# The front of a three-layer kernel, emitted from a list of nodes instead of a hand-written step table

## The chip, the cores and the metric

One core of a Trainium2 chip runs the whole program. Its engines work side by side, each through its own row of instructions in a fixed order: TensorE (PE: matmul and transpose, results go to PSUM), VectorE (DVE), ScalarE (ACT), GpSimd (POOL) and the queue engine SyncE (SP). An instruction that waits holds up everything behind it on its engine. The metric is the device time of one execution in microseconds. The runs shown have a median of 1156.69 us (1154.55 to 1157.05).

## What is computed

Three layers follow each other. A long convolution by Fourier transform over 8 batches of 3072 tokens with 256 channels; a mixture of 8 experts, where each token goes to the expert with the largest logit as long as that expert has room (768 places); and a feed-forward layer with softplus. Tokens that found no room are rows of zeros for the last layer.

```python
X = np.fft.rfft(x, axis=1)
y = np.fft.irfft(X * F, n=x.shape[1], axis=1)
...
expert_idx = np.argmax(logits, axis=1)
gate_w = probs[np.arange(N), expert_idx]
for i in range(N):
    e = expert_idx[i]
    if counts[e] < capacity:
        disp[e, counts[e]] = x[i]
h = np.maximum(np.einsum('ecd,edf->ecf', disp, w1), 0.0)
y = np.einsum('ecf,efd->ecd', h, w2)
...
h = x @ w_in
g = np.maximum(h, 0.0) + np.log1p(np.exp(-np.abs(h)))
return (g @ w_out).astype(np.float32)
```

## The kernel before

Only the first three batches are transformed unless an expert still has room after them. The transform of a batch is four matrix stages. Batch 0 keeps stage 1 on the chip (`x1`, `tr1`); batches 1 and 2 write it to memory (`x1_out`, tile `s`, buffer `mid`) and read it back reordered (`load_i`, tile `it`). `s2` is the second stage: two matmuls into a PSUM tile of the ring `y`, three VectorE products with the filter (L237 to L240), and a GpSimd sum (L241). `s3` is the third stage, whose result ScalarE copies into the tile `e`. `gsum`, `gturn` and `gate` make the logits, the gate weights `ga` and the place of each token. `tr2` and `s4` do the last stage and scale it, and `park` writes the rows to memory (`rowsd`).

`table` turns the places of a batch into an index table by one-hot matmuls. It has four chunks. For each, VectorE compares into `lo` and `hv` (L369, L370), GpSimd multiplies `hv` by the token numbers (L371), TensorE does eight matmuls (L375), and VectorE adds the result into `ts` (L377). There is one buffer of `lo` and of `hv`.

After that come 16 units of 384 places, two for each expert. A unit gathers its rows (`load_x`), transposes them (`tr_x`, tiles `xh`, `xl`), and does `w1`, `w2` in eight tasks each, with every operand split in a high and a low part. The result `yh`, `yl` goes through 16 softplus steps: `wi` (six matmuls into `pi`, L593), three ScalarE instructions, a VectorE sum `g` (L496), a split into `gh`, `gl`, and `wo` (nine matmuls, L616). `wih`, `wil`, `woh`, `wol` are the last layer's weights, which arrive as 64-bit numbers. 16 conversions (`split_res`) turn them into 32-bit numbers and split them. A conversion is five VectorE instructions (L473 to L481) with a ScalarE instruction between the third and the fourth. Its scratch is a PSUM tile (`pv`) as long as a ring is given, and an SBUF tile (`wv`) after that.

The program is recorded as it is written, so the order of the calls is the order in each engine's row. The order is a hand-written table of steps: `ev(t, order, fn)` puts a call on step t, and step 0 is the first softplus step. Batch b starts at step -71 plus 0, 17 or 29, and each function has a fixed offset from there. Most functions hold their TensorE part and the copy of its result together. Memory is handed over in rooms: `x_done`, `make_room`, `low_room` and `finish` close the pools of the transform and open those of the units.

Of the kernel before, what the change touches and what calls it, by code (L numbers as in the profile page):

```python
# [25 lines left out]
WI0 = 4  # L26
STATIC = 3

# [68 lines left out]

def body(tc, cap, x, ff, fx, wg, w1, w2, win, wout, m1, m2, m4, small, out):
# [25 lines left out]
    wexp = sm[0:N1, 576:832].rearrange("p (n e) -> p n e", e=E)  # L124
    eoff = sm[0:N1, 832:840]
    tok1 = sm[0:N1, 840:872]
    iota = sm[0:N1, 872:]
# [4 lines left out]
    slead = const.tile([128, nblk], F32, name="slead")  # L132
    flag = const.tile([1, 1], I32, name="flag")
# [4 lines left out]
    class Conv:  # L138


        def __init__(self, st, ste, stf, stx, tag):
# [18 lines left out]
            self.ga = {}  # L160
            self.e = {}
# [12 lines left out]
        def make_m3(self, q):  # L174
            ps = psa.tile([128, 4, 128], F32, name="p0", tag="a")
            for i in range(4):
                nc.tensor.transpose(ps[:, i], self.m2s[:, 4 * q + i], ident)
            nc.scalar.copy(self.m3s[:, 4 * q:4 * q + 4], ps)
# [11 lines left out]
        def x1(self, b, g, h):  # L190

            if g == 0 and h == 0:
                self.d = self.ep[1].tile([128, 2, N1, N2], F32, name="d", tag="e1")
            xt = self.xt[b, g]
            ps = psa.tile([128, 4, N1], F32, name="p1", tag="a")
            for i in range(4):
                nc.tensor.matmul(ps[:, i], lhsT=xt[:, i, 128 * h:128 * h + 128], rhs=self.m1s, start=True, stop=True)
            (nc.scalar.copy, nc.vector.tensor_copy)[h](
                self.d[:, h, :, 4 * g:4 * g + 4].rearrange("c q n -> c n q"), ps)

        def tr1(self, b, k):

            ps = psa.tile([128, 2, 2, 128], F32, name="p2", tag="a")
            for i in range(2):
                for h in range(2):
                    p = 2 * k + i
                    nc.tensor.transpose(ps[:, i, h], self.d[:, h, 4 * p:4 * p + 4].rearrange("c r n -> c (r n)"), ident)
            self.it[b, k] = self.ip.tile([128, 2, D], F32, name="it", tag="it")
            nc.scalar.copy(self.it[b, k], ps.rearrange("p i h c -> p i (h c)"))

        def x1_out(self, b, g):

            xt = self.xt.pop((b, g))
            t = self.sp.tile([N1, 4, D], F32, name="s1", tag="s1")
            for i in range(2):
                ps = psa.tile([N1, 2, D], F32, name="p8", tag="a")
                nc.tensor.matmul(ps.rearrange("q n c -> q (n c)"), lhsT=self.m1s,
                                 rhs=xt[:, 2 * i:2 * i + 2].rearrange("p n c -> p (n c)"), start=True, stop=True)
                nc.scalar.copy(t[:, 2 * i:2 * i + 2], ps)
            nc.scalar.dma_start(mid[b - 1].rearrange("(q n) c -> q n c", n=N2)[:, 4 * g:4 * g + 4], t)  # L220
# [6 lines left out]
        def s2(self, b, k):  # L227

            p0 = 2 * k
            it = self.it.pop((b, k))  # L230
            ps = psy.tile([128, 2, D], F32, name="p3", tag="y")
            for i in range(2):
                nc.tensor.matmul(ps[:, i], lhsT=self.m2s[:, p0 + i], rhs=it[:, i], start=True, stop=True)
# [6 lines left out]
            nc.vector.tensor_tensor(out=t2[64:128], in0=ps[0:64], in1=fi, op=ALU.mult)  # L240
            nc.gpsimd.tensor_tensor(out=z, in0=z, in1=t2, op=ALU.add)  # L241
            self.z[b, k] = z

        def s3(self, b, k):

            if k == 0:
                self.e[b] = self.ep[b % 2].tile([128, 2, N1, N2], F32, name="e", tag=f"e{b % 2}")
            z = self.z.pop((b, k))
            ps = pso.tile([128, 2, 2, 128], F32, name="p4", tag="o")
            for i in range(2):  # L250
                for h in range(2):
                    nc.tensor.matmul(ps[:, h, i], lhsT=z[:, i, 128 * h:128 * h + 128], rhs=self.m3s[:, 2 * k + i],
                                     start=True, stop=True)
            nc.scalar.copy(self.e[b][:, :, 8 * k:8 * k + 8].rearrange("c h q n -> c h (q n)"),
                           ps.rearrange("c h i x -> c h (i x)"))

        def tr2(self, b, m):

            ps = psa.tile([N1, 4, 128], F32, name="p5", tag="a")
            for i in range(4):  # L260
                nc.tensor.transpose(ps[:, i], self.e[b][:, i % 2, :, 2 * m + i // 2], ident)
            self.jt[b, m] = self.jp.tile([N1, 2 * D], F32, name="j", tag="j")
            (nc.vector.tensor_copy if b == STATIC - 1 and m % 2 else nc.scalar.copy)(
                self.jt[b, m], ps.rearrange("p a c -> p (a c)"))

        def gsum(self, b):

            gx = self.gp.tile([128, N1, 8], F32, name="gx")
            for half in range(2):
                ps = pso.tile([128, N1 // 2, 8], F32, name="pg", tag="o")  # L270
                qs = slice(48 * half, 48 * half + 48)
                for hc in range(2):
                    for j in range(4):
                        nc.tensor.matmul(ps[32 * j:32 * j + 32], lhsT=self.wgs[:, hc],
                                         rhs=self.e[b][:, hc, qs, 8 * j:8 * j + 8],
                                         start=(hc == 0), stop=(hc == 1), skip_group_check=True)
                (nc.vector.tensor_copy, nc.scalar.copy)[half](gx[:, qs], ps)
            self.gx = gx

        def gturn(self, b):  # L280

            self.gsb[b] = self.gp.tile([N1, N2, E], F32, name="gsb", tag="gsb")
            gv = self.gsb[b].rearrange("p (j t a) e -> p t a j e", t=2, a=4)
            for t in range(2):
                ps = psa.tile([N1, 4, 128], F32, name="p7", tag="a")
                for a in range(4):
                    nc.tensor.transpose(ps[:, a], self.gx[:, :, 4 * t + a], ident)
                nc.vector.tensor_copy(gv[:, t], ps.rearrange("p a (j x) -> p a j x", x=32)[:, :, :, 0:E])

        def s4(self, b, m):  # L290

            g, i0 = m // 2, m % 2 * 2
            if i0 == 0:
                self.yt[b, g] = self.yp.tile([N1, 4, D], F32, name="yt", tag="yt")
            ps = pso.tile([N1, 2, D], F32, name="p6", tag="o")
            nc.tensor.matmul(ps.rearrange("p a c -> p (a c)"), lhsT=self.m4s, rhs=self.jt.pop((b, m)),
                             start=True, stop=True)
            for i in range(2):
# [3 lines left out]
        def gate(self, b):  # L302


            gp = self.gp
            pl = pso.tile([N1, N2, E], F32, name="pl", tag="o")
            nc.tensor.matmul(pl.rearrange("p n e -> p (n e)"), lhsT=self.m4s,
                             rhs=self.gsb[b].rearrange("p n e -> p (n e)"), start=True, stop=True)
            mx = gp.tile([N1, N2], F32, name="mx")
            nc.vector.tensor_reduce(out=mx, in_=pl, axis=AXL.X, op=ALU.max)  # L310
            dl = gp.tile([N1, N2, E], F32, name="dl")
            nc.vector.tensor_tensor(out=dl, in0=pl, in1=mx.unsqueeze(2).to_broadcast([N1, N2, E]), op=ALU.subtract)
# [695 lines left out]
```

## Time and profile before

| what | value |
|---|---|
| profiled execution | 1156.95 us, span of the trace 1154.8 us |
| TensorE busy, mean granted clock | 1071.3 us (93%), 0.958 |
| ScalarE, GpSimd, VectorE busy | 780.4 us (68%), 600.5 us (52%), 488.2 us (42%) |
| HBM over the span | 102 GB/s |
| first softplus matmul | 343.5 us |

The busy share of TensorE is an average over two halves, the front before the first softplus step and the units after it, and has to be read for each. Matmuls are pipelined, so their durations overlap: the work of a task is the time from its start to the start of the next. A granted clock of 1.00 is 2.4 GHz, of 0.50 it is 1.2 GHz.

### The profile page before, as it was taken

How to read it: one execution, taken by the hardware profiler on the slowest of the kernel's cores; microseconds unless marked ns; L12 is line 12 of the kernel's file. 1: busy time of each engine (PE TensorE's matmuls, PEld its weight loads, DVE VectorE, ACT ScalarE, POOL GpSimd, SP SyncE). 2: the span in 40 equal slices, each digit the busy share in tenths (PEclk: the TensorE clock that was granted, in tenths of full speed). 3: DMA queues.
4: the chain of work that ended last, by engine and by line, in shares of the span. 5: the costliest groups of instructions: out<-in, count | busy, mean ns of one | idle time of the engine just before them, and what ended most of it. 6: DMA issues, size and time to landing. Idle time of an engine off the chain costs nothing. (4 is left out here: it accounts for less than half of the span.)

```text
span 1154.8 us, 18098 instructions
## 1 busy us (share of the span) xinstructions
PE 1071.3 (93%) x6704; PEld 994.9 (86%) x6704; DVE 488.2 (42%) x848; ACT 780.4 (68%) x1618; POOL 600.5 (52%) x548
## 2 busy tenths in 40 slices
PE   9999876865878999999999999999999999999994
PEld 7746664533778999999999999999999999999994
DVE  4538876465765364332333333333232333232221
ACT  3656332652557878777787878787777777777883
POOL 0313423242566555567657475665757566554553
PEclk9999887877899999999999999999999999999997
DMA  9977321453351124543323233333211122100000
GB/s 280 276 221 224 106 69 37 127 169 101 114 174 51 37 60 152 200 136 120 119 101 128 93 128 106 114 106 115 65 46 65 51 60 60 51 15 11 14 15 16
DMA packets 71953, 119.30 MB, mean 103 GB/s; under 512 B 6832, under 2 KB 45872, under 8 KB 71856
## 3 DMA queue, kind: packets, MB, share of 16 engines
q1 hardware_dynamic: 58032, 89.74, 24.2%
q10 hardware_dynamic: 9216, 15.73, 4.4%
q0 software_dynamic: 4608, 12.59, 3.3%
q8 instruction: 54, 0.88, 0.3%
q14 instruction: 43, 0.35, 0.1%
HBM read 70.85 MB, written 47.19 MB: 102 GB/s over the span
## 5 line engine op out<-in xcount | busy, mean ns | idle before, releaser
L496 DVE SCALAR_TENSOR_TENSOR g<-pi,ln 128x384 f32<-128x384 f32 x256 | 142.7, 557 | 509.5 <-ACT ln L491 469.5
L408 POOL TENSOR_TENSOR gl<-g,gh 128x384 fp32r<-128x384 f32 x256 | 259.8, 1019 | 117.2 <-ACT gh L407 90.1
L616 PE MATMUL po<-woh,gh 128*128 128x256 f32 x768 | 219.1, 285 | 2.7 <-DVE ot L623 1.3
L616 PE MATMUL po<-wol,gh 128*128 128x256 f32 x768 | 217.0, 282 | 0.0
L616 PE MATMUL po<-woh,gl 128*128 128x256 f32 x768 | 216.6, 282 | 0.0
L488 ACT ACTIVATE ab<-pi 128x384 f32<-128x384 f32 x256 | 124.4, 486 | 124.9 <-PE pi L593 118.8
L593 PE MATMUL pi<-yh,wih 128*128 128x384 f32 x512 | 172.7, 337 | 5.1 <-DVE g L496 5.1
L593 PE MATMUL pi<-yh,wil 128*128 128x384 f32 x512 | 173.9, 340 | 0.0
L593 PE MATMUL pi<-yl,wih 128*128 128x384 f32 x512 | 172.8, 338 | 0.0
L408 POOL TENSOR_TENSOR w1l<-ws,w1h 128x512 fp32r<-128x512 f32 x64 | 83.5, 1305 | 154.1 <-ACT w1h L407 151.8
L616 PEld LDWEIGHTS po<-woh,gh 128*128 128x128 f32 x768 | 145.0, 189 | 3.7 <-ACT ab L488 1.9
L616 PEld LDWEIGHTS po<-wol,gh 128*128 128x128 f32 x768 | 145.6, 190 | 0.0
L616 PEld LDWEIGHTS po<-woh,gl 128*128 128x128 f32 x768 | 145.5, 189 | 0.0
L491 ACT ACTIVATE ln<-ab 128x384 f32<-128x384 f32 (+1 forms) x257 | 135.0, 525 | 8.2
L489 ACT ACTIVATE ab<-ab 128x384 f32<-128x384 f32 (+1 forms) x257 | 134.7, 524 | 8.1
L407 ACT CAST gh<-g 128x384 fp32r<-128x384 f32 x256 | 130.0, 508 | 0.3 <-DVE g L496 0.3
L241 POOL TENSOR_TENSOR z<-z,t 128x512 f32<-128x512 f32 x36 | 52.8, 1468 | 138.8 <-DVE t L240 97.0
L408 POOL TENSOR_TENSOR w2l<-ws,w2h 128x512 fp32r<-128x512 f32 x64 | 82.8, 1294 | 56.7 <-ACT w2h L407 55.3
L593 PEld LDWEIGHTS pi<-yh,wih 128*128 128x128 f32 x512 | 96.9, 189 | 5.9 <-DVE g L496 5.9
L565 ACT ACTIVATE hh<-pw 128x384 fp32r<-128x384 f32 x128 | 63.0, 492 | 53.8 <-PE pw L561 53.8
L593 PEld LDWEIGHTS pi<-yh,wil 128*128 128x128 f32 x512 | 96.9, 189 | 0.0
L578 PE MATMUL py<-hh,w2h 128*128 128x384 f32 x256 | 89.8, 351 | 7.5 <-DVE yl L585 7.5
(148 smaller groups left out, 2030.8 us busy)
## 6 DMA issues: line engine op xcount, KB each, us to landing
ws<-in_w_dram SPq DMA_DIRECT2D x128, 256.0 KB, 2.8
out_dram<-cs SPq DMA_DIRECT2D x48, 512.0 KB, 3.8
xt<-in_x_dram SPq DMA_DIRECT2D x24, 384.0 KB, 8.4
mid<-s ACTq DMA_DIRECT2D x16, 384.0 KB, 3.3
it<-mid ACTq DMA_DIRECT2D x24, 256.0 KB, 3.2
rowsd<-yt SPq DMA_DIRECT2D x16, 384.0 KB, 3.2
wst<-in_win_dram SPq DMA_DIRECT2D x8, 512.0 KB, 5.5
wst<-in_wout_dram SPq DMA_DIRECT2D x8, 512.0 KB, 4.0
```

The source lines that it names most:

```text
L241: nc.gpsimd.tensor_tensor(out=z, in0=z, in1=t2, op=ALU.add)
L407: nc.scalar.copy(dst_hi, src)
L408: nc.gpsimd.tensor_tensor(out=dst_lo, in0=src, in1=dst_hi.bitcast(F32), op=ALU.subtract)
L488: nc.scalar.activation(out=ab[:, :n], in_=h, func=ACTF.Abs)
L489: nc.scalar.activation(out=ab[:, :n], in_=ab[:, :n], func=ACTF.Exp, scale=-1.0)
L491: nc.scalar.activation(out=ln[:, :n], in_=ab[:, :n], func=ACTF.Ln, bias=1.0)
L496: nc.vector.scalar_tensor_tensor(out=g[:, :n], in0=h, scalar=0.0, in1=ln[:, :n], op0=ALU.max, op1=ALU.add)
L565: nc.scalar.activation(out=hh, in_=ps, func=ACTF.Relu)
L578: nc.tensor.matmul(self.py[d], lhsT=a[:, j % 2, ds], rhs=b, start=(j == 0 and n == 0), stop=(j == 7 and n == 2))
L593: nc.tensor.matmul(self.pi, lhsT=a[i // 2][:, i % 2, k], rhs=b[:, k], start=(n == 0), stop=(n == 5))
L616: nc.tensor.matmul(self.po[t], lhsT=a[:, ts], rhs=b[:, i], start=(i == 0 and n == 0), stop=(i == KI - 1 and n == 2))
```

## The change

The part of the program before the first softplus step is no longer a table of steps. Each call becomes a node with an engine, a cost in ns, its predecessors, the buffer rings it takes and gives back, and the bytes it moves. `Plan.order` walks through the list when the program is built: it keeps a clock for each engine, for the transfers and for the port of VectorE and GpSimd, and places next the node that can start first (starts within 60 ns of the engine's clock count as equal), of equals the one with the longest chain behind it. `LIFT` is a table of lengths added for ten groups of nodes. The functions are cut so that a TensorE part and the copy of its result are separate nodes. The table gets eight chunks with two sets of `lo` and `hv` that live in the constants; `wexp` is broadcast instead of stored. `woh` and `wol` go into the left room together, and the tiles `yh`, `yl` take the low room. Conversions that the plan starts after the end of its TensorE nodes are put on steps of the second half, with SBUF scratch.

```diff
+QT = 8
...
+    BUFS = {"a": 3, "y": 2, "o": 3, "it": 4, "z": 3, "t2": 2, "j": 4, "yt": 3, "xt": 8, "s1": 2, "e0": 1, "e1": 1,
+            "gx": 1, "gsb": 1, "lo": 2, "wst": 3, "wf": 2, "ws": 5, "w1h": 3, "w2h": 3, "xd": 3, "x": 2, "h": 4, "Y": 3}
...
+    def add(self, name, engine, cost, fn, after=(), take=(), give=(), nbytes=0, lock=False, tail=0, behind=()):
+        assert name not in self.node
+        self.node[name] = (engine, cost, fn, list(after), list(take), list(give), nbytes, lock, tail, list(behind))
...
+        while ready:
+            best = None
+            for n, r in ready.items():
+                f = free[node[n][0]]
+                t = when(n, max(r, f))
+                if t is None:
+                    continue
+                if node[n][7]:
+                    t = max(t, port)
+                key = max(t, f + 60), -length[n]
+                if best is None or key < best[0]:
+                    best = key, n, t
...
+            start[n], free[e] = t, t + cost
+            done[n] = t + cost + self.HOP[e]
+            if lock:
+                port = t + cost
+            if nbytes:
+                bus = max(bus, t + cost + 1200) + nbytes / 285
+                done[n] = bus + 600
...
-            for q in range(4):
-                ns = slice(8 * q, 8 * q + 8)
...
-                ps = psa.tile([128, nblk], F32, name="p9", tag="a")
-                for j in range(8):
-                    nc.tensor.matmul(ps, lhsT=lo[:, j], rhs=hv[:, j], start=(j == 0), stop=(j == 7))
...
+        def table_d(self, b, q):
...
+            n = N2 // QT
+            lo, hv = onehot[q % 2]
+            ns = slice(n * q, n * q + n)
+            for row, w, to in ((0, 128, lo), (1, nblk, hv)):
+                nc.vector.tensor_tensor(out=to, in0=iota[:, 0:w].unsqueeze(1).to_broadcast([N1, n, w]),
+                                        in1=ij[b][:, row, ns].unsqueeze(2).to_broadcast([N1, n, w]), op=ALU.is_equal)
...
+        def table_p(self, b, q):
+            n = N2 // QT
+            lo, hv = onehot[q % 2]
+            ps = self.ps["t", b, q] = psa.tile([128, nblk], F32, name="p9", tag="a")
+            for j in range(n):
+                nc.tensor.matmul(ps, lhsT=lo[:, j], rhs=hv[:, j], start=(j == 0), stop=(j == n - 1))
...
+            for k in range(12):
+                load(("it", b, k), lambda b=b, k=k: cv.load_i(b, k), 256, "ACT",
+                     after=[("mid", b, g) for g in range(8)], take=["it"],
+                     behind=[("it", b, k - 1) if k else ("tr1", 11) if b == 1 else ("it", b - 1, 11)])
...
+                add(s2, "PE", 862, lambda b=b, k=k: cv.s2(b, k), after=[("it", b, k), ("m2", k // 2)], take=["y"],
+                    give=[("it", ("it", b, k) if b else ("tr1", k))], behind=prev("s2"))
+                add(tf, "DVE", 2070, lambda b=b, k=k: cv.times_f(b, k), after=[s2, ("f", k // 2)], take=["z", "t2"],
+                    give=[("y", s2)], behind=prev("tf"))
...
+            for q in range(QT):
+                td, th, tp, tt = (T((q, i)) for i in range(4))
+                add(td, "DVE", 1050, lambda b=b, q=q: cv.table_d(b, q), take=["lo"], lock=True,
+                    after=[T((q - 1, 0))] if q else [G(8)] + ([("t", b - 1, 4)] if b else []))
+                add(th, "POOL", 500, lambda b=b, q=q: cv.table_h(b, q), after=[td], lock=True)
+                add(tp, "PE", 450, lambda b=b, q=q: cv.table_p(b, q), after=[th], take=["a"], give=[("lo", td)])
...
+        TURN, res_space = 6, [psy, pso]
...
+            due = 33000 - 4200 * n
+            add(("c", n, 0), "DVE", 2070, stage(), after=[("r", n), *room], take=["y" if n < TURN else "o", "wf"], tail=due,
+                behind=[("c", n - 1, 2)] if n else [])
...
+        order = plan.order(plan.LIFT)
+        assert len(order) == len(plan.node)
+        end = max(plan.done[n] for n in order if plan.node[n][0] == "PE")
+        rest_of = [n for n in order if plan.start[n] > end and n[0] in ("c", "r")]
+        for n in order:
+            if n not in rest_of:
+                plan.node[n][2]()
+        res_space[:] = [None, None]
...
+        for n in rest_of:
+            t = int((plan.start[n] - end) * 1.75 // 3200)
...
+            ev(t, AHEAD - 0.5, plan.node[n][2])
```

TensorE, the table of batch 1 and the last second-stage tasks of batch 2 (`p<-it,m2s`), before:

```order
L252 MATMUL p_1544<-m3s,z 128x128 x4
L375 MATMUL p_1558<-hv,lo 128x48 x8
L233 MATMUL p_1568<-it,m2s 128x256 x2
L296 MATMUL p_1577<-j,m4s 96x512
L261 MATMUL p_1581<-sm,e 96x128 x4
L261 MATMUL p_1588<-sm,e 96x128 x4
L252 MATMUL p_1595<-m3s,z 128x128 x4
L375 MATMUL p_1607<-hv,lo 128x48 x8
L233 MATMUL p_1617<-it,m2s 128x256 x2
```

The same place now, from the last third-stage task of batch 2 (`p<-m3s,z`) on:

```order
L371 MATMUL p_1666<-m3s,z 128x128 x4
L423 MATMUL p_1675<-j,m4s 96x512
L423 MATMUL p_1720<-j,m4s 96x512
L384 MATMUL p_1725<-sm,e 96x128 x4
L384 MATMUL p_1732<-sm,e 96x128 x4
L397 MATMUL pg<-e,wgs 32x384 x16
L515 MATMUL p_1775<-hv_83,lo_82 128x48 x4
L515 MATMUL p_1780<-hv_85,lo_84 128x48 x4
L423 MATMUL p_1790<-j,m4s 96x512
```

The matmuls of table 1 stood in front of second-stage tasks of batch 2. They now stand behind all of them and behind the gate sum of batch 2, in halves from two sets of tiles.

VectorE at the same place before, with the compares (`lo`, `hv`), the small sums (`ts`) and the products with the filter (`z`, `t`):

```order
L369 TENSOR_TENSOR lo<-sm,ij 96x1024
L370 TENSOR_TENSOR hv<-sm,ij 96x384
L379 COPY ts<-p_1558 128x48
L237 TENSOR_TENSOR z<-p_1568,fr 128x512
L238 SCALAR_TENSOR_TENSOR t_1572<-p_1568,fi 64x512
L240 TENSOR_TENSOR t_1572<-p_1568,fi 64x512
L369 TENSOR_TENSOR lo<-sm,ij 96x1024
L370 TENSOR_TENSOR hv<-sm,ij 96x384
```

VectorE now, from the last products of batch 2 on:

```order
L355 TENSOR_TENSOR z<-p_1581,fr 128x512
L356 SCALAR_TENSOR_TENSOR t_1601<-p_1581,fi 64x512
L358 TENSOR_TENSOR t_1601<-p_1581,fi 64x512
L525 TENSOR_TENSOR slot<-slot,ts 128x48
L526 SCALAR_TENSOR_TENSOR ts<-ts,base 128x48
L528 TENSOR_TENSOR slot<-slot,ts 128x48
L529 TENSOR_SCALAR base<-base 128x1
L489 CAST ix<-ixf 96x32
L490 TENSOR_SCALAR ix<-ix 96x32
L491 TENSOR_SCALAR ix<-ix 96x32
L492 CAST ij_80<-ix 96x64
L612 TENSOR_SCALAR pv<-wst 128x512
```

Each small sum stood right behind its compares and in front of the next products. The products of batch 2 now end first, then the slots of batch 0 and the index `ij` of batch 1 are made, and the first conversion (`pv`) follows ahead of the compares of table 1.

VectorE at the first softplus sums (`g`) before, with `hl` of the unit two ahead and the conversions:

```order
L496 SCALAR_TENSOR_TENSOR g<-pi,ln 128x384
L566 SCALAR_TENSOR_TENSOR hl<-pw,hh 128x384
L496 SCALAR_TENSOR_TENSOR g<-pi,ln 128x384
L479 SCALAR_TENSOR_TENSOR pv<-wst,pv 128x512
L481 SCALAR_TENSOR_TENSOR wf<-wf,pv 128x512
L473 TENSOR_SCALAR wv<-wst 128x512
L474 SCALAR_TENSOR_TENSOR wf<-wst,wv 128x512
L475 TENSOR_SCALAR wv<-wst 128x512
L496 SCALAR_TENSOR_TENSOR g<-pi,ln 128x384
```

And now:

```order
L643 SCALAR_TENSOR_TENSOR g<-pi,ln 128x384 x2
L735 SCALAR_TENSOR_TENSOR hl<-pw,hh 128x384
L618 SCALAR_TENSOR_TENSOR wv<-wst,wv 128x512
L620 SCALAR_TENSOR_TENSOR wf<-wf,wv 128x512
L612 TENSOR_SCALAR wv<-wst 128x512
L613 SCALAR_TENSOR_TENSOR wf<-wst,wv 128x512
L614 TENSOR_SCALAR wv<-wst 128x512
L643 SCALAR_TENSOR_TENSOR g<-pi,ln 128x384 x2
```

One conversion had its scratch in SBUF (`wv`) before; now the last five have it, and the second part of one and the first part of the next stand together between two sums.

## Rows read from the trace of the kernel before

**Rows 1.** Busy time by stretch: us, PE, PEld, DVE, ACT, POOL, PEclk, DMA share, GB/s

```profile
0.00:82.25 82.25, 78.68 (x457) 56.09 (x458) 35.04 (x59) 40.99 (x69) 15.44 (x16) 1.00 0.89 263
82.25:343.20 260.95, 203.33 (x1000) 152.56 (x999) 180.82 (x300) 115.48 (x243) 98.97 (x78) 0.85 0.41 127
100.00:125.00 25.00, 24.82 (x150) 19.06 (x148) 21.82 (x30) 16.13 (x36) 12.87 (x9) 1.00 0.70 220
300.00:343.20 43.20, 30.95 (x166) 29.26 (x165) 34.53 (x62) 24.65 (x49) 28.83 (x24) 0.93 0.53 177
343.20:375.00 31.80, 27.68 (x152) 27.16 (x151) 16.88 (x24) 22.47 (x47) 20.02 (x17) 0.88 0.16 47
375.00:1100.00 725.00, 721.92 (x4816) 719.90 (x4815) 243.64 (x443) 567.86 (x1191) 440.89 (x412) 1.00 0.25 86
```

**Rows 2.** Waits of PE from 82.25 to 343.2: total us, times, longest

```profile
PE p L375 <- POOL hv L371: 31.1, 10, 5.7
```

**Rows 3.** Tile pi: duration ns min/median/max, first and last start us

```profile
L593 PE MATMUL pi<-yh,wih x512: 332/336/523, 343.5 to 1134.3; 128*128 128x384 f32 x171
```

**Rows 4.** PE in order of time: start us, us, what

```profile
6.50 14.43 PE L197 MATMUL p<-m1s,xt 96*128 96x96 f32 x128
20.76 0.60 PE L177 MATMUL p<-sm,m2s 128*128 128x128 f32 x4
...
103.67 1.06 PE L252 MATMUL p<-m3s,z 128*128 128x128 f32 x8
104.57 1.03 PE L233 MATMUL p<-it,m2s 128*128 128x256 f32 x4
105.43 1.88 PE L296 MATMUL p<-j,m4s 96*96 96x512 f32 x4
107.15 1.04 PE L261 MATMUL p<-sm,e 128*96 128x128 f32 x8
108.03 1.06 PE L252 MATMUL p<-m3s,z 128*128 128x128 f32 x8
108.84 1.05 PE L375 MATMUL p<-hv,lo 96*128 96x48 f32 x8
109.73 1.11 PE L233 MATMUL p<-it,m2s 128*128 128x256 f32 x4
...
297.65 0.33 PE L561 MATMUL pw<-xh,w1h 128*128 128x384 f32 x1
...
298.69 0.33 PE L578 MATMUL py<-hh,w2h 128*128 128x384 f32 x1
```

**Rows 5.** DVE in order of time, first product of batch 1

```profile
82.25 0.69 DVE L237 TENSOR_TENSOR z<-p,fr 128x512 f32<-128x512 f32 x1 [3.43 <-PE p L233]
```

**Rows 6.** DMA issues: KB each, median us from issue to landing

```profile
mid<-s ACTq DMA_DIRECT2D x16, 384.0 KB, 3.3
it<-mid ACTq DMA_DIRECT2D x24, 256.0 KB, 3.2
```

**Rows 7.** Groups of DVE instructions: busy us, mean ns, idle before

```profile
L370 DVE TENSOR_TENSOR hv<-sm,ij 96x384 fp32r<-96x384 f32 x12 | 14.1, 1172 | 0.0
L473 DVE TENSOR_SCALAR pv<-wst 128x512 uint32<-128x512 uint32 x15 | 10.3, 686 | 0.0
L346 DVE TENSOR_TENSOR v<-v,dl 96x256 f32<-96x256 f32 x3 | 1.3, 422 | 0.1
```

**Rows 8.** Tile hv: duration ns min/median/max

```profile
L370 DVE TENSOR_TENSOR hv<-sm,ij x12: 546/1614/1623, 105.5 to 286.6; 96x384 fp32r<-96x384 f32 x12
```

**Rows 9.** Tile wv, the one conversion with scratch in SBUF

```profile
L473 DVE TENSOR_SCALAR wv<-wst x1: 1973/1973/1973, 355.7 to 355.7; 128x512 uint32<-128x512 uint32 x1
L474 DVE SCALAR_TENSOR_TENSOR wf<-wst,wv x1: 1566/1566/1566, 357.8 to 357.8; 128x512 f32<-128x512 uint32 x1
...
L481 DVE SCALAR_TENSOR_TENSOR wf<-wf,wv x1: 1666/1666/1666, 363.8 to 363.8; 128x512 f32<-128x512 f32 x1
```

**Rows 10.** Waits from 340 to 376 us, the row of PE for the softplus sum

```profile
PE pi L593 <- DVE g L496: 4.1, 2, 3.0
```

More of the change, by code (lines that the diff above doesn't have):

```diff
@@ L260, in tr2, with tr2_j @@
             for i in range(4):
                 nc.tensor.transpose(ps[:, i], self.e[b][:, i % 2, :, 2 * m + i // 2], ident)
+        def tr2_j(self, b, m, vector):
             self.jt[b, m] = self.jp.tile([N1, 2 * D], F32, name="j", tag="j")
[L263 to L278, printed above, removed]
@@ new lines, in gsum @@
+        def gsum(self, b, half):
+            ps = self.ps["gs", b, half] = pso.tile([128, N1 // 2, 8], F32, name="pg", tag="o")
+            qs = slice(48 * half, 48 * half + 48)
+            for hc in range(2):
+                for j in range(4):
+                    nc.tensor.matmul(ps[32 * j:32 * j + 32], lhsT=self.wgs[:, hc],
+                                     rhs=self.e[b][:, hc, qs, 8 * j:8 * j + 8],
+                                     start=(hc == 0), stop=(hc == 1), skip_group_check=True)
@@ new lines, in load_const, with step_of, fn @@
+        def load_const(which):
+            if which:
+                cv.load_m4()
+                nc.sync.dma_start(sm[:, 128:], small[:, 128:])
+                cv.load_wg()
+            else:
+                nc.sync.dma_start(ident, small[:, 0:128])
+        def step_of(gens, b, make):
+            def fn():
+                if b not in gens:
+                    gens[b] = make()
+                next(gens[b], None)
+            return fn
+        load("m1", lambda: nc.sync.dma_start(cv.m1s, m1), 36, tail=10 ** 6)
@@ new lines, in body, with first @@
+        add("warm", "PE", 4500, warm, take=["z", "a"], give=[("z", "warm"), ("a", "warm")])
+        seq = ["m1"]
+        def first(name, fn, kb, **k):
+            load(name, fn, kb, behind=[seq[-1]], tail=10 ** 6, **k)
+            seq.append(name)
+        for g in range(8):
+            first(("x", 0, g), lambda g=g: cv.load_x(0, g), 384, take=["xt"])
+        first("ident", lambda: load_const(0), 64)
+        for g in range(6):
+            first(("m2", g), lambda g=g: cv.load_m2(g), 256)
+            first(("f", g), lambda g=g: cv.load_f(g), 768)
+            if g >= 2:
+                first(("x", 1, g - 2), lambda g=g: cv.load_x(1, g - 2), 384, take=["xt"])
@@ L762, in x_done, with keep @@
+        def keep():
+            nc.vector.tensor_copy(clead, ctot)
+            nc.vector.tensor_copy(slead, slot)
+        add("keep", "DVE", 350, keep, after=[("g", STATIC - 2, 6), ("t", STATIC - 2, 4)])
+        last = STATIC - 1
+        parks = [[("park", b, g) for g in range(8)] for b in range(STATIC)]
         def x_done():
@@ L764, in x_done, with make_room @@
             wi_pools(stw, "M")
-            for _ in range(3):
-                load_next()
+        def make_room():
+            stf.close()
+            right_pools(stw, "M")
         def low_room():
```

697 lines of the change are left out of this document (442 added, 255 removed).

## The prediction

> **What bounds the kernel now.** I read the busy time of each engine by stretch first [rows 1]. The program has two halves. From 343.2 us on, TensorE repeats softplus steps: between 375 and 1100 us it is busy 721.92 of 725.00 us at full clock, 4816 matmuls, 6.64 in a microsecond. That half is bound by TensorE, and the change takes no matmul out of it. Before 343.2 lies the front. Up to 82.25 us it is dense too (78.68 of 82.25 us, granted clock 1.00). In the 260.95 us after that TensorE is busy 203.33 us and the granted clock is 0.85 of 2.4 GHz, so part of the busy time is work at 1.2 GHz. No other engine is full there: VectorE has 180.82 us (69%), ScalarE 115.48, GpSimd 98.97, DMA a share of 0.41. So the front from 82 to 343 us is bound by waits, and the waits of TensorE come next [rows 2]: 31.1 us, in 10 waits, are for `hv`, the one-hot tile of the table that VectorE makes and GpSimd multiplies. The reader is to see one engine that waits for a chain through two others, with other work standing behind the wait in its own row. The first matmul of the second half starts at 343.5 us [rows 3]; the forecast is about when it starts afterwards.
>
> **What the front costs TensorE without waits.** Durations overlap, so I take start to start at full clock [rows 4]. The 16 tasks of stage 1 of batch 0 take 20.76 - 6.50 = 14.3 us. A task of four transposes takes (108.03 - 107.15) / 2 = 0.44; there are 72 (6 for m3, 12, 48 and 6): 31.7. The second stage takes 105.43 - 104.57 = 0.86, 36 times: 31.0. The third 104.57 - 103.67 = 0.90, 36 times: 32.4. A matmul 512 wide takes (107.15 - 105.43) / 2 = 0.86; 32 in stage 1 of the other batches and 48 in stage 4: 68.8. A table chunk of eight takes 109.73 - 108.84 = 0.89; 12 of them, or 24 halves, 10.7. A w1 or w2 task takes 298.69 - 297.65 = 1.04, 35 times: 36.4. The three gate sums of 32 short matmuls I estimate from stage 1's row (14.43 us for 128) at 3.6 each: 10.7; the rest at 4. Sum 240.0, and the first task starts at 6.50: the first step could start at 246.5 us. Of the 343.5 us, 97 us are waits and slow clock. No edit changes these counts; the list orders them anew.
>
> **VectorE is the second floor.** The first VectorE product of batch 1 starts at 82.25 us [rows 5], and I leave this anchor there: in the new row TensorE has about 82 us of the same work in front of it, and before it batch 1 must go to memory and come back, 3.3 and 3.2 us [rows 6] after the last of its stage 1, which stands some 11 us of TensorE work earlier. Up to the first step VectorE now does 35.04 + 180.82 = 215.9 us. In the new order 11 first halves and 10 second halves of the weight conversions stand ahead of the first softplus sum, against 14 and 13: five instructions of 0.69 us [rows 7] three times, 10.3 us less. The table costs more: the same columns in 24 pairs instead of 12. Row `hv` takes 0.546 us at best and 1.172 on average [rows 7, 8], so a pair carries about 0.63 us of waiting; 12 more pairs make 7.5 us, and I estimate 5 us for the doubled fixed cost and the 12 more small sums. That makes 218. Ahead of the anchor the new row puts what is left of batch 0's gate (17 short instructions at about 0.42 [rows 7], 7 us) and two half pairs (2.4 us), into time in which VectorE was idle. 173 us are left after the anchor. Without a gap the last of it ends at 255 us, 9 us above TensorE's floor. The densest row of before has VectorE at 21.82 of 25.00, 87% [rows 1]; 173 at 87% is 198, which ends at 280. The new order runs the six or more products of a batch in one piece and has table, conversion and gate work ready between, which speaks for the upper end, and both engines being close to full with fixed rows speaks against it. I take the middle: the first step at 268 us.
>
> What hides what: the table chunks stay as dear as they were for VectorE, but TensorE has two sets of one-hot tiles and stage 4, or w1, in between, so the 31.1 us go. What is late next is VectorE itself, in the last 50 us ahead of the first step, where `xl`, `hl`, table 2 and six conversions share it. The table of batch 1 is placed behind the last product of batch 2, no longer in front of it, so it becomes the path to the gathers; about 100 of the 173 us come before its end, so VectorE has it near 185 us, the gather lands some 6 us later, and TensorE reaches the first gathered tile no earlier than 194. It costs nothing unless VectorE slips by more than 3 us, and from there one for one, which is what the gap between the floors and the forecast is for. Splitting each function into a TensorE part and a copy part costs no instruction. The smaller constant load saves 0.1 MB of transfer and nothing on the path.
>
> **What the second half pays.** Five conversions now fall behind the first step, with their scratch in SBUF instead of PSUM; before there was one. That one shows the price: 1973, 1566 and 1666 ns for three of its five instructions [rows 9], against 686 with the scratch in PSUM [rows 7]. While it ran GpSimd was busy, and TensorE waited 4.1 us for VectorE's sum `g` in those steps [rows 10]. By its row the old kernel loses there: 152 matmuls in 31.80 us [rows 1] are worth 152 / 6.64 = 22.9 us, so 8.9 us are lost. Five conversions of about 6.3 us are 31 us of VectorE. They fall into 14 steps of 21 matmuls, 294 / 6.64 = 44 us, of which VectorE's own work takes 34% (243.64 of 725.00), so 29 us are free. The loss lies between 3 us (all hidden) and 20 (4.1 for each); I take 12, which is 3 more than now.
>
> The Trainium skill, page "SBUF — State Buffer", section "Who interferes with whom", says that VectorE and GpSimd share one port pair as an exclusive lock, that a VectorE instruction with two SBUF inputs contends with a GpSimd one that reads SBUF, and that the loser waits for the whole instruction. The trace agrees: `hv` is either 0.55 or 1.61 us long [rows 8]. By that rule the change pays twice, since it doubles the instructions of this kind in the table and takes the conversions out of PSUM; a rival below carries it.
>
> **Sum.** 268.0 for the front, 811.3 from the first step to the end of the span (1154.8 - 343.5), 3.0 more there: 1082.3. The profiled execution took 1156.95, 2.15 outside the span, which stays: 1084.5, say 1085. It lies 0.3 above the median of the runs shown, 1156.69, so the gain is 72 us.
>
> **Rivals.** (1) VectorE runs without a gap and the conversions hide: first step at 255, second half 6 us shorter than now: 1062. For it speaks that TensorE's own floor, 246.5, lies below that; against it, that no row of before shows VectorE that dense.
> (2) VectorE holds only the 80% of the stretch just ahead of the first step, 34.53 of 43.20 us [rows 1], which holds the same mix of `hl`, `xl` and conversions: 173 / 0.80 = 216, first step at 299, end at 1115. For it speaks that these rows are in order and wait for ScalarE's round trip; against it, that the mix fills only the last fifth.
> (3) VectorE's one-hot instructions meet GpSimd at work each time: all 48 wait the whole 1.07 us (1614 - 546) [rows 8] instead of 24 times 0.63 on average. That is 36 us more, 209 us of VectorE; at the density of the forecast (173 in 186) 225 us, first step at 307, second half 11 longer: 1131. For it speaks that the median of the row is the long time; against it, that the mean, 1.172, is that of some seven long and five short ones. It is the skill's lock rule, read for every instruction.
> (4) Slower than before: ScalarE's row. The 24 loads of `it` stand in it between the copies that empty PSUM, and each waits there for a store of `mid` or a free buffer; everything behind it waits, and TensorE for that. If each held the row for one landing of 3.3 us [rows 6], 79 us are added to 268, and the second half loses 11: 1171. It decides from 2.8 us for each load; below that the kernel is still faster. For it speaks that four loads stand right behind the last store; against it, that the rest find their data landed long before, and ScalarE has over 50% of the front free.
>
> **Chances.** Forecast 0.55, its own range 1070 to 1102; (1) 0.17; (2) 0.14; (3) 0.07; (4) 0.05; 0.02 for a gain lost altogether. Below 1060 I leave some 0.06, above 1120 about 0.12. The range is 1060 to 1120. This kernel's runs tell 0.2%, 2.3 us, from no change: faster 0.93, same 0.02, slower 0.05.
>
> **What would show it.** First `pi` matmul between 255 and 285 us; granted clock between 82 us and there above 0.93; VectorE's share there 87% or more and TensorE's wait for `hv` under 8 us in all. The second half's first 14 steps would show the `wv` rows five times, with 1 to 2 us where GpSimd runs, and TensorE waiting for `g`. The forecast is wrong if VectorE's share stays near 70% with the first step past 300, if ScalarE waits on DMA for more than 10 us, or if the second half takes over 825 us.

## The result, and the profile after

The changed kernel takes 1084.87 us (median of 4 runs, 1083.80 to 1085.58), the kernel before 1155.62 beside it: a ratio of 0.9387, 95% interval 0.937 to 0.9404. The forecast was 1085. The profiled execution took 1083.8 us, 1.9 of it outside the span of 1081.9. One execution of each kernel is profiled, and the granted clock differs a little between executions (0.987 to 0.990 over these four), so idle time compares better between profiles than the start of the first step.

Where the time went is read from busy time by stretch, with the columns of [rows 1]; 266.0 is the first softplus step:

```profile
0.00:85.78 85.78, 81.70 (x487) 59.16 (x488) 42.58 (x79) 45.70 (x82) 16.82 (x18) 1.00 0.87 254
85.78:266.00 180.22, 169.41 (x971) 127.89 (x970) 162.38 (x301) 107.77 (x224) 91.01 (x85) 0.99 0.57 174
0.00:266.00 266.00, 251.11 (x1457) 187.05 (x1458) 204.97 (x379) 153.47 (x305) 107.83 (x103) 0.99 0.66 199
212.00:265.80 53.80, 49.81 (x281) 44.22 (x280) 51.47 (x100) 33.39 (x69) 36.12 (x35) 1.00 0.57 173
266.00:310.00 44.00, 38.80 (x224) 37.35 (x223) 29.76 (x42) 33.96 (x70) 28.60 (x23) 0.92 0.27 81
310.00:1024.00 714.00, 711.02 (x4730) 709.05 (x4729) 244.78 (x440) 558.46 (x1172) 438.43 (x409) 1.00 0.26 86
```

Put the third line beside the sum of the two front lines of [rows 1]. Both fronts have 1457 matmuls. Before, TensorE was busy 78.68 + 203.33 = 282.0 us of 343.2 and idle for 61.2. Now it is busy 251.1 of 266.0 and idle for 14.9. So of the 77 us of front, 46 are idle time that is gone, and 31 are the same matmuls done in less time: the granted clock from 82 us on was 0.85 and is 0.99 from 85.78 on. Busy time times clock hardly changes: 78.68 x 1.00 + 203.33 x 0.85 = 251.5 before, 81.70 x 1.00 + 169.41 x 0.99 = 249.4 now. In these rows, the waits and the clock go together.

The first `pi` matmul, 343.5 us in [rows 3], and TensorE's longest waits up to it (total, times, longest), where [rows 2] had 31.1 us for `hv`:

```profile
L777 PE MATMUL pi<-yh,wih x512: 332/338/522, 266.0 to 1060.3; 128*128 128x384 f32 x171
```

```profile
PE p L515 <- DVE j L388: 3.0, 1, 3.0
PE p L515 <- POOL hv L507: 1.9, 2, 1.3
PE p L863 <- DVE z L860: 1.6, 1, 1.6
PE p L325 <- ACT s L331: 1.4, 1, 1.4
PE p L384 <- DVE ts L520: 1.1, 1, 1.1
```

The rest are below 1 us each. What is left of the idle time is many short gaps, the longest of them 3.0 us. That one has a cause nobody looked for. VectorE's and GpSimd's rows around it, in order of time:

```profile
191.87 1.13 DVE L463 TENSOR_TENSOR oh<-v,vm 96x256 f32<-96x256 f32 x1
193.04 4.43 DVE L466 TENSOR_TENSOR_SCAN rk<-sm,oh 96x256 f32<-96x256 f32 x1
197.50 0.17 DVE L470 COPY cn<-rk 96x8 f32<-96x8 f32 x1
197.59 0.69 DVE L388 COPY j<-p 96x512 f32<-96x512 f32 x1
```

```profile
192.50 0.74 POOL L507 TENSOR_TENSOR hv<-hv,sm 96x192 fp32r<-96x192 f32 x1
193.21 1.26 POOL L675 TENSOR_TENSOR w1l<-ws,w1h 128x512 fp32r<-128x512 f32 x1
194.44 1.27 POOL L675 TENSOR_TENSOR w2l<-ws,w2h 128x512 fp32r<-128x512 f32 x1
195.67 1.25 POOL L631 TENSOR_TENSOR wil<-wf,wih 128x512 fp32r<-128x512 f32 x1
```

The scan takes 0.69 us in its two other places. Here it starts inside a run of GpSimd instructions without a gap (its last four are shown) and ends half a microsecond after the last of them. `j` stands behind it, and TensorE waits for `j`: the table's matmuls (L515) take a PSUM tile of the ring that this copy empties.

Behind the first step, the five conversions with scratch in SBUF, against 686 ns with PSUM scratch [rows 7] and the one of before [rows 9] (duration ns min/median/max):

```profile
L612 DVE TENSOR_SCALAR wv<-wst x5: 417/419/428, 272.4 to 310.2; 128x512 uint32<-128x512 uint32 x5
L613 DVE SCALAR_TENSOR_TENSOR wf<-wst,wv x5: 692/693/1668, 272.9 to 310.7; 128x512 f32<-128x512 uint32 x5
L614 DVE TENSOR_SCALAR wv<-wst x5: 426/1126/1406, 273.6 to 312.4; 128x512 uint32<-128x512 uint32 x5
L618 DVE SCALAR_TENSOR_TENSOR wv<-wst,wv x5: 681/691/2798, 278.3 to 314.3; 128x512 uint32<-128x512 uint32 x5
```

From 266 to 310 us TensorE does 224 matmuls, at the later pace (4730 in 714 us, 6.62 in one) 33.8 us of work: 10.2 us are lost, with the clock at 0.92. From the first step to the end of the span it is 815.9 us, 811.3 before.

### The profile page after: what moved, and what is told of

It reads as the page before. It is cut to its first block, busy times and chain, and to the rows that moved or that the text cites. A ratio compares the mean times of both kernels' runs of the same rounds, so it can differ in the third digit from the quotient of the medians.

```text
span 1081.9 us, 18177 instructions
## 1 busy us (share of the span) xinstructions
PE 1042.6 (96%) x6704; PEld 974.6 (90%) x6704; DVE 491.7 (45%) x884; ACT 781.3 (72%) x1618; POOL 600.7 (56%) x560
## 4 chain that ended last, share of the span: by engine, by line
PE 81%; DVE 7%; DMA 4%; ACT 2%; issue 2%; POOL 2%; SPq 0%; POOLq 0%; DVEq 0%
PE pi L777 24%; PE po L800 23%; PE pw L723 11%; PE py L752 11%; PE p L423 2%; PE p L325 2%; DMA xt<-in_x_dram 2%; PE p L346 1%; PE p L384 1%; PE p L371 1%; POOL gl L552 1%; DMA fr<-in_ff_dram 1%; PE pt L700 1%; PE pg L397 1%; DMA mid<-s 1%
## 5 line engine op out<-in xcount | busy, mean ns | idle before, releaser
L800 PE MATMUL po<-woh,gh 128*128 128x256 f32 x768 | 216.3, 282 | 2.7 <-ACT ab L635 1.3
L777 PEld LDWEIGHTS pi<-yl,wih 128*128 128x128 f32 x512 | 96.6, 189 | 0.0
L363 POOL TENSOR_TENSOR z<-z,t 128x512 f32<-128x512 f32 x36 | 46.9, 1304 | 86.4 <-DVE t L358 66.1
```

The lines of the kernel that those rows point to most:

```text
L777: nc.tensor.matmul(self.pi, lhsT=a[i // 2][:, i % 2, k], rhs=b[:, k], start=(n == 0), stop=(n == 5))
L800: nc.tensor.matmul(self.po[t], lhsT=a[:, ts], rhs=b[:, i], start=(i == 0 and n == 0), stop=(i == KI - 1 and n == 2))
```

## The experiments

The theory under test is the prediction's: the order of the list removes TensorE's waits, and VectorE is what is late next. Rivals: the new table alone does it; any list would do; TensorE itself, not VectorE, now sets the end of the front. Each kernel ran beside the kernel before on the same chip; the changed kernel is the reference point at 1084.87 us, ratio 0.9387.

**The new table in the old order.** In the kernel before, the edit in words:

```
-for q in range(4):    lo, hv of eight columns, one buffer each
+for q in range(9):    chunk q's lo, hv of four columns, two buffers each,
+                      and then the matmuls of chunk q - 1
```

> The kernel before, its hand-written order kept, with the table alone taken from the change: eight chunks of four columns, two sets of one-hot tiles, each chunk's tiles made one step ahead of its matmuls. If the order of the list is what gave the gain, this keeps most of the time before: of TensorE's 31.1 us of waits for hv [rows 2] up to half go, for 1140 to 1152 us, a ratio of 0.986 to 0.997. If the table's two sets are what gave it, half or more of the 71 us comes: 1120 us or less.

1142.1 us, ratio 0.989 (0.986 to 0.992). In the profile, of an execution of 1148.03 us, TensorE still waits 22.5 us for `hv`, and the first step comes at 333.8 us:

```profile
0.00:333.80 333.80, 282.08 (x1456) 208.78 (x1457) 225.74 (x394) 156.70 (x312) 117.27 (x106) 0.89 0.54 164
```

Busy time and clock are as before (282 us, 0.89). The table alone is worth 13 of the 71 us. Shown: the table in the old order does not give the rest. The list, the cut functions and the moved rooms came together, and no run separates them.

**The list by another rule.**

```
-                key = max(t, f + 60), -length[n]
+                key = max(t, f + 60), list(node).index(n)
...
-            assert n[0] == "r" or t < (2 * n[1] if n[1] < KI // 2 else 2 * n[1] - KI + 4), n
+            t = t if n[0] == "r" else min(t, (2 * n[1] if n[1] < KI // 2 else 2 * n[1] - KI + 4) - 1)
```

> The changed kernel with another rule of choice in the list scheduler: among nodes that could start equally early it takes the one declared first, not the one with the longest way to the end. If the gain hangs on the order that the path lengths give, waits of TensorE come back and the first pi matmul starts at 285 to 305 us instead of 266, for 1103 to 1125 us. If any order that a list scheduler makes out of the waits would do, the time stays within 5 us of 1085.

The second part caps the steps of the late conversions. 1105.81 us, ratio 0.9581 (0.9551 to 0.961), in the range of the first theory, with the first step at 282.1, 3 us ahead of its range. This other list, which also plans around the waits, keeps some 49 us; the path lengths with their table of additions bring the other 21.

```profile
0.00:282.10 282.10, 258.94 (x1457) 188.92 (x1458) 197.18 (x374) 152.61 (x303) 107.10 (x102) 0.97 0.62 186
```

In the front TensorE is idle 8 us longer than in the changed kernel, and the same matmuls take 8 us longer. From the first step to the end of the span it is 821.8 us, 5.9 more, with six conversions behind the first step, not five.

**One set of one-hot tiles, the list kept but for that.**

```
-            lo, hv = onehot[q % 2]
+            lo, hv = onehot[0]
...
-        order = plan.order(plan.LIFT)
+        order = one_set(plan, plan.order(plan.LIFT))   # a chunk's tiles wait for the matmuls before
```

> The changed kernel with one set of one-hot tiles: the list is the same, except that a chunk's tiles are made only after the matmuls of the chunk before it, and what hangs on them moves along. Theory: 21 times VectorE waits for TensorE and GpSimd where it now works ahead; since other work stands between most chunks in the list, a third of them cost 0.5 to 1 us: 1088 to 1093 us. Rival, the second set is most of the gain: 1105 us or more. Rival, it does nothing under a list: within 2 us of 1085.

1098.99 us, ratio 0.9519 (0.9495 to 0.9542): 14 us, between the two expectations. The first step is at 281.5:

```profile
0.00:281.50 281.50, 260.72 (x1456) 192.16 (x1457) 201.09 (x379) 153.63 (x305) 106.24 (x103) 0.96 0.62 188
```

```profile
PE p L515 <- POOL hv L507: 8.5, 7, 2.9
```

I had priced the waits and left out the clock: idle time grew by 5.9 us to 20.8, busy time by 9.6 at a clock of 0.96 instead of 0.99.

**Eight copies from VectorE to ScalarE, and the reverse.** The list is that of the changed kernel; only the engine of `j<-p` in the third batch changes.

```
-                    lambda b=b, m=m, vec=vec: cv.tr2_j(b, m, vec)
+                    lambda b=b, m=m: cv.tr2_j(b, m, False)              # all on ScalarE
+                    lambda b=b, m=m: cv.tr2_j(b, m, b == STATIC - 1)    # all sixteen on VectorE
```

> The changed kernel in its own order, with the eight copies j<-p of the third batch that VectorE makes (0.68 us each, between 190 and 218 us) made by ScalarE instead (0.58 us each). If VectorE sets when the front ends, its row is 5.4 us shorter there and the first pi comes 2 to 5 us earlier: 1080 to 1083 us. If TensorE alone sets it, nothing moves: 1084 to 1086. If ScalarE has no room there either (it has 36.5 of 46.6 us busy between 165 and 212), it gets 1 to 4 us slower: 1086 to 1089.

> The counterpart to the run that moved eight copies to ScalarE (1078.7 us): all sixteen copies j<-p of the third batch on VectorE, in the changed kernel's own order. VectorE gets 5.5 us more between 187 and 226 us and ScalarE 4.7 us less. If VectorE sets the end of the front, the first pi comes 3 to 7 us later than 266.0: 1087 to 1092 us. If the gain of that run was ScalarE's doing, or a scan that happened not to be held up, the time stays within 2 us of 1085 or falls.

On ScalarE: 1078.72 us, ratio 0.9342 (0.9317 to 0.9367), just clear of the changed kernel's interval: about 6 us faster, and no version that was run is measurably faster than it. First step at 262.0; TensorE's busy time is the same, the idle time 4 us less:

```profile
0.00:262.00 262.00, 251.09 (x1456) 188.09 (x1457) 197.65 (x371) 156.48 (x313) 107.84 (x103) 0.99 0.67 202
```

On VectorE: 1089.12 us, ratio 0.9425 (0.9398 to 0.9452), first step at 271.9, TensorE's waits for `j` 5.3 us:

```profile
0.00:271.90 271.90, 256.01 (x1456) 189.71 (x1457) 209.03 (x387) 149.43 (x297) 107.47 (x103) 0.98 0.66 195
```

Idle time is 1.0 us longer than in the changed kernel, busy time 4.9. Part of the 4.9 is not the edit's: between 85 and 110 us, ahead of every copy that was moved, the granted clock is 0.93 here and in the run on ScalarE, and 1.00 in the changed kernel's profile. The scan was held in neither (0.75 and 0.69 us at most). Both moved as the theory has it, but both touch the one VectorE instruction TensorE waits for, so they don't yet say that VectorE's load as a whole is the bound.

**VectorE's load taken away.** In the eleven conversions ahead of the first step:

```
-        if f64:
+        if f64 and space is not None:
+            f = t.bitcast(F32).rearrange("p (f two) -> p f two", two=2)[:, :, 1]
+            yield 0
+            yield 1
+            yield 2
+        elif f64:
```

> The changed kernel without VectorE's and ScalarE's part in putting the float64 weights together in the eleven conversions ahead of the first softplus step (the weights' upper words are taken as they are, so the output is not the reference's): VectorE has 36 us less to do there, the list and everything else stay. If VectorE is what is last at the end of the front, the first pi moves towards TensorE's own busy time, 251 us: 1069 to 1077 us. If TensorE alone sets it, the gain is 2 us or less. If VectorE alone did all along, with TensorE's work fitting in, 25 us or more go: under 1060.

1089.01 us, ratio 0.9435 (0.9409 to 0.946): slower, which no theory had. The loaded tile now stays in use until GpSimd's subtraction, and the weight loads behind it on SP's queue came late:

```profile
POOL xd L695 <- DMA ws<-in_w_dram: 9.4, 1, 9.4
ACT yt L432 <- DMA rowsd<-yt: 8.1, 1, 8.1
ACT w1h L675 <- DMA ws<-in_w_dram: 5.2, 1, 5.2
```

That decides nothing about VectorE, so it was done again with a copy of the tile:

```
...
+            f = P.wl.tile([128, 512], F32, name="wf", tag="wf")
+            yield 0
+            nc.scalar.copy(f, t.bitcast(F32).rearrange("p (f two) -> p f two", two=2)[:, :, 1])
+            yield 1
...
```

> The question of the run without VectorE's work in the front's conversions again, without that run's flaw (the loaded tile stayed in use until GpSimd's subtraction, so the loads behind it on SP's queue came late). Here ScalarE makes one copy of the upper words (0.62 us, in place of its 0.66 us step), and the loaded tile is free after it, earlier than in the changed kernel; VectorE has 36 us less to do ahead of the first pi, and no PSUM bank is taken for scratch (the output is again not the reference's). If VectorE is what ends last in the front, the first pi comes at 253 to 260 us instead of 266.0 and the time is 1072 to 1079 us. If TensorE sets the end (251.1 us busy, and its 14.9 us of gaps stand at other places), VectorE is felt at single places only, yl at the end and j behind the scan: first pi at 262 to 266, 1081 to 1085 us.

The first step comes at 265.4 us in the profile, against 266.0:

```profile
0.00:265.40 265.40, 253.06 (x1456) 189.40 (x1457) 171.65 (x326) 153.34 (x305) 108.85 (x103) 0.98 0.66 200
212.00:265.40 53.40, 51.72 (x295) 46.37 (x294) 32.73 (x70) 34.98 (x73) 37.41 (x35) 1.00 0.60 189
```

VectorE has 33 us less to do up to the first step (171.65 against 204.97) and is busy 61% of the last 53 us, where it had 96% (51.47 of 53.80); the front ends 0.6 us earlier. TensorE's idle time falls by 2.6 us, from 14.9 to 12.3, and its busy time rises by 1.9, at a clock of 0.98. The wait for `j` behind the held scan is there unchanged (3.0 us, the scan 4.44). So 12.3 of the 14.9 us of gaps stand without that work, and the first step lies in the rival's range. The times are less clear: the median of 5 runs, 1078.89 us (1077.43 to 1081.81), lies in the range of the other expectation, and its ratio, 0.9343 (0.9319 to 0.9368), is just clear of the changed kernel's. The profiled execution took 1081.49. Of the 6.0 us in the medians the profiles show 0.6 in the front and 1.6 behind the first step. So the front as a whole is not VectorE's; where the other 4 us come from, and how much of them is VectorE's, stays open.

**The late conversions without their work**, the first of these two edits with `space is None`:

> The changed kernel without the same work in the five conversions behind the first softplus step, whose scratch lies in SBUF (again the upper words as they are). The stretch from 265.8 to 310 us does 225 matmuls where the steady rows behind it do 6.62 per us, so 10 us are lost there. If these conversions are what delays g on VectorE, 6 to 10 us go: 1075 to 1079 us. If the loss is that of the softplus steps running up, whatever VectorE does, 1082 to 1086.

1076.45 us, ratio 0.9324 (0.9298 to 0.9349); from the first step, at 266.7, to the end of the span 808.3 us, 7.6 less. Stretches of 45 us, 0.3 us behind the first step here and from the first step on in the changed kernel:

```profile
267.00:312.00 45.00, 43.55 (x282) 42.94 (x281) 14.57 (x27) 38.97 (x83) 31.23 (x29) 1.00 0.28 85
```

```profile
266.00:311.00 45.00, 39.80 (x230) 38.35 (x229) 30.72 (x44) 34.51 (x71) 29.39 (x24) 0.92 0.26 79
```

Again a pair of effects: 3.8 us of idle time go, and the clock stays at 1.00. The rival, the steps' running up, is out as the main cause.

**GpSimd's subtractions as fills.**

```
-            nc.gpsimd.tensor_tensor(out=lo, in0=self.ws.pop(i), in1=hi.bitcast(F32), op=ALU.subtract)
+            nc.gpsimd.memset(lo.bitcast(F32), 0.0)      # units 0, 1 and the early pieces of 2
```

> The changed kernel with GpSimd's twenty subtractions w1l and w2l of the front (1.3 us each) replaced by fills with zero, which have no operand to read (the low halves of the first units' weights are left out of the result). If these subtractions are what holds VectorE's long instructions in the last 75 us before the first pi, the scan at 193 us takes 0.69 us instead of 4.43, lo at 246 us under 1 us instead of 2.99, and the first pi comes 3 to 6 us earlier: 1078 to 1082 us. If the holding costs nothing, because TensorE has other work meanwhile, the time stays within 1.5 us of 1085 though the scan is short.

1081.05 us, ratio 0.9365 (0.9343 to 0.9386), which overlaps the changed kernel's. The scan takes 0.69 us everywhere, `lo` 1.42 at most instead of 2.99. The first step comes 1.3 us earlier (264.7), where 3 to 6 were expected; the wait for `j` went, and one of 2.3 us for the gathered tiles came. That the subtractions hold VectorE is shown; that this costs the time is not shown by the times.

**Three tries at a better version**, each with the eight copies on ScalarE:

```
+        order.remove(("c", 10, 0))                                          # first and second try
+        order.insert(order.index(("yl", 1, 1)) + 1, ("c", 10, 0))
...
-            t = int((plan.start[n] - end) * 1.75 // 3200)                   # first try
+            t = int((plan.start[n] - end) * 2.1 // 3200)
...
-        res_space[:] = [None, None]                                         # third try
+        res_space[:] = [psa, psa]
```

> A version meant to beat both: the eight copies j<-p on ScalarE (1078.7 us by itself), yl of the second unit ahead of the first three instructions of the eleventh conversion on VectorE, which now stand between hl and yl, and the steps of the last five conversions spread over the first softplus steps by a fifth more. TensorE's gaps at the end of the front (0.7 us for yl, 0.5 us for hl) go, and where the conversions stand closest, from 281 to 291 us, their 2.8 us instructions come one step apart: 2 to 4 us in all, for 1074 to 1077 us. If the loss behind the first pi hangs on the holding of single instructions, wherever they stand, the spreading gives nothing: 1077 to 1079.

> One part of the last version alone: the eight copies on ScalarE (1078.7 us by itself) and yl ahead of the first three instructions of the eleventh conversion; the last conversions stand where the changed kernel has them. If the 4.81 us wv of that version, held while GpSimd ran gl, wol, w2l and gl without a gap, came from the spreading, it goes, and TensorE's 0.7 and 0.5 us at the end of the front too: 1077 to 1078.5 us. If any shift of the rows makes another instruction meet such a run of GpSimd, 1079 to 1083 again.

> The eight copies on ScalarE (1078.7 us by itself), and the scratch of the last five conversions in PSUM, in the ring of three banks that pi, pw and pt use, instead of in SBUF. If what is lost behind the first pi is VectorE held by GpSimd while all its operands lie in SBUF, L612, L614 and L618 take 0.7 us each as in the front, TensorE's waits for g (6.1 us in 262 to 320 us) fall under 2 us, and 4 to 7 us go: 1072 to 1075 us. Rival: a bank that is scratch for 4 to 5 us is missed by pi, whose steps take 3 us, and TensorE waits for it: 1079 to 1090.

They took 1080.89, 1080.89 and 1078.56 us (ratios 0.9371, 0.9361 and 0.9343, each about 0.002 to 0.003 wide to either side): none is measurably faster than the 1078.72 (ratio 0.9342) they start from. In the first two the move meant to help cost more than it gave: TensorE waits 2.6 us for `hl`, in place of 0.7 for `yl` and 0.5 for `hl`. Behind `yl` the conversion stands ahead of `hl` of the third unit, and TensorE has that unit's first w2 task ahead of `pi` (the second try's row):

```profile
262.59 0.44 PE L752 MATMUL py<-hl,w2h 128*128 128x384 f32 x1 [2.59 <-DVE hl L735]
```

In the first try another instruction met a run of GpSimd. VectorE's and GpSimd's rows:

```profile
269.96 0.42 DVE L612 TENSOR_SCALAR wv<-wst 128x512 uint32<-128x512 uint32 x1
270.49 0.69 DVE L613 SCALAR_TENSOR_TENSOR wf<-wst,wv 128x512 f32<-128x512 uint32 x1
271.21 4.81 DVE L614 TENSOR_SCALAR wv<-wst 128x512 uint32<-128x512 uint32 x1
275.94 1.01 DVE L643 SCALAR_TENSOR_TENSOR g<-pi,ln 128x384 f32<-128x384 f32 x2
```

```profile
271.35 1.01 POOL L552 TENSOR_TENSOR gl<-g,gh 128x384 fp32r<-128x384 f32 x1
272.30 1.27 POOL L631 TENSOR_TENSOR wol<-wf,woh 128x512 fp32r<-128x512 f32 x1
273.53 1.25 POOL L675 TENSOR_TENSOR w2l<-ws,w2h 128x512 fp32r<-128x512 f32 x1
274.75 0.98 POOL L552 TENSOR_TENSOR gl<-g,gh 128x384 fp32r<-128x384 f32 x1
```

TensorE waited 4.81 us for `g` there. The spreading only changed which instruction is hit: in the second try it was L618 at 275.88 us with 2.80, as in the changed kernel. In the third, with PSUM scratch, no conversion is held at all (all sixteen, the late ones too):

```profile
L613 DVE SCALAR_TENSOR_TENSOR wf<-wst,pv x16: 686/687/690, 168.1 to 307.0; 128x512 f32<-128x512 uint32 x16
L614 DVE TENSOR_SCALAR pv<-wst x16: 694/695/706, 168.9 to 307.8; 128x512 uint32<-128x512 uint32 x16
```

The clock is 1.00 from 261 to 310 us, and yet nothing is gained: in the 44 us from the first step on TensorE does 227 matmuls, and 228 in the run with the eight copies alone. TensorE now also waits ahead of `pt` and `pw`, which take banks of the ring that the scratch is in; that is how the rival had it, though the rows name only VectorE as the releaser:

```profile
PE pi L777 <- DVE g L643: 3.0, 2, 1.7
PE pt L700 <- DVE g L643: 1.6, 1, 1.6
PE pw L723 <- DVE g L643: 1.2, 1, 1.2
PE pi L777 <- DVE hl L735: 1.2, 1, 1.2
```

## Why the prediction was right, and where its reasons were not

- **TensorE's waits go, the clock rises.** As forecast: 31.1 us for `hv` became 1.9 (under 8 was set as the test), the clock from 85.78 us on is 0.99 (above 0.93).
- **First step at 268.** It is 266.0. The way there was wrong, though: the step "What is late next is VectorE itself", with VectorE's work after the anchor at a density of 87 to 100%. The profile fulfils the sign I had set for it, 162.38 of 180.22 us, 90%; but with 33 us of that work gone the profiled front ended 0.6 us earlier, and 12.3 of 14.9 us of idle time stayed. A busy share of 90 or 96% was no bound. By its sum the front is TensorE's, 251.1 us of work and 14.9 of short gaps; no run took work off TensorE to show it. My floor for that work was too low as well. From the first task of stage 1 on TensorE is busy 246.6 us, at a clock of 0.99, where I had summed 240.0 at full clock:

```profile
6.12:266.00 259.88, 246.59 (x1452) 185.07 (x1451) 204.31 (x374) 152.19 (x304) 107.63 (x99) 0.99 0.66 200
```

That puts the floor at 252.7 us instead of 246.5 and leaves 13.3 us of gaps to 266.0, where I had left 21.5 to 268. A floor that was too low and a delay that was too long nearly cancelled; to that extent the hit was luck. Two slips in the working change nothing: 173 us at 87% end at 281 us, not 280, and 0.86 us is what a pair of matmuls 512 wide takes, so the 80 are pairs.
- **The anchor at 82.25** came at 85.78 us, and VectorE did 205.0 us of work up to the first step, not 218: 48 one-hot instructions took 20.5 + 14.0 us, `hv` mostly its short 0.35. After the anchor 162 us were left instead of 173, which made up for the later start.
- **The table's path to the gathers.** I had table 1 end near 185 us and TensorE reach the gathered tile at 194; they came at 201 and 208.28. I had priced such a slip "one for one" from 3 us on. TensorE's row shows no wait for the gathered tiles, since the list had other work in front of them; its one gap at these transposes, 0.57 us, is put down to a copy `j`. This step failed without harm.
- **Second half.** Forecast 814.3 us from the first step, 12 lost at its head; measured 815.9 and 10.2. The cause is the one named: without the five conversions' work 7.6 us come back. A part of the price is the clock (0.92), which the estimate had only because it was taken from a row that held it too, 0.88 in [rows 1]. That the price hangs on scratch in SBUF, as [rows 9] was read, is not shown: with scratch in PSUM nothing was gained. And the head alone does not make the difference to the kernel before, 4.6 us where 3.0 was forecast: it loses 10.2 us against 8.9. The 712.5 us behind it hold 12 matmuls fewer (4721 against 4733, 1.8 us at 6.62 in one), and the end from the last `pi` task on takes 21.6 us against 20.5; neither has a cause here.
- **Rivals.** ScalarE's row waits for no DMA worth naming (its longest sums are 28.1 us for `p` of line 371 and 15.5 for line 423, both TensorE's). The gapless VectorE and the thin one both assumed that VectorE decides. The lock at every one-hot instruction did not come, with a median of 0.35 us for `hv`; the lock came elsewhere, and longer.

## What to carry to other kernels

A wait of TensorE can cost more than its length: with one set of one-hot tiles 5.9 us more idle time put the first step 15.5 us later, since the matmuls ran at a granted clock of 0.96 instead of 0.99, and 31 of the 77 us that the front lost were such busy time. It need not: with the eight copies on ScalarE 4.0 us less idle time gave 4.0 us. A busy share near full shows a candidate, not the bound; take its work away (without changing when its inputs are released) and see whether the end moves. Where rows are fixed in order, look for single instructions that TensorE waits for directly: eight copies on another engine took 4.0 us of idle time from TensorE, 33 us less work elsewhere on the same engine 2.6.

## What was not expected of the hardware

VectorE was held not for one GpSimd instruction but for a whole run of them: 4.43 us for the scan (0.69 alone), 2.99 for `lo` (0.68), 2.80 for `wv` at L618 (0.69), 4.81 at L614 (0.43), each ending within 0.6 us of the end of a run of GpSimd instructions without a gap. Among the held are instructions with two SBUF inputs and a `TENSOR_SCALAR` with one; the sixteen conversions with PSUM scratch were never held (706 ns at most). The Trainium skill, page "SBUF — State Buffer", section "Who interferes with whom", says, of VectorE's 2-port modes, that whoever issues first has the shared pair for the whole instruction; these rows go further, since, as they read, GpSimd's next instruction got ahead of a VectorE instruction that was already waiting. Why it does, no run here shows.
